# Bucket attention with a dense layer behind it: the first batch attended in one pass, its weights turned by TensorE's transpose

## The chip, the cores and the metric

The kernel runs on one core of a Trainium2 chip. The metric is the device time of one execution in microseconds (us). Three runs of the kernel before took 904.26, 904.30 and 908.95 us; their median is 904.3 us.

## What is computed

Four batches of eight heads, 768 tokens, 64 channels per head. A token sees only the tokens whose queries or keys fall into the same of 64 hash buckets; the attended values of all heads, 512 wide, go through a dense layer with GELU and a second dense layer.

```python
q_bits = (np.einsum('bhsd,dk->bhsk', q, proj) > 0)   # k_bits likewise, six bits each
mask = q_bucket[:, :, :, None] == k_bucket[:, :, None, :]
scores = np.where(mask, 0.125 * np.matmul(q, k.transpose(0, 1, 3, 2)), -1e9)
attn = np.exp(scores - np.max(scores, axis=-1, keepdims=True))
attn = attn / (np.sum(attn, axis=-1, keepdims=True) + 1e-09)
x = np.matmul(attn, v).transpose(0, 2, 1, 3).reshape(3072, 512)
h = x @ w_in                                         # 512 x 2048
return (0.5 * h * (1 + erf(h / sqrt(2)))) @ w_out    # 2048 x 512
```

## The kernel before

**Order of the work.** The kernel is a list of steps, each with an engine (or several to choose from), a cost, a key (smaller is sooner), the steps it needs and the buffer ring it takes. `Plan.order` (L94) simulates the engines and fixes the order in which each engine's instructions are written; the table `PAR` (L33) holds the numbers that shift the keys. At run time each engine works through its own list in that order and waits where a needed step is late.

**A unit** (`unit`, L748) is 128 queries of one head against all 768 keys; there are 192. TensorE (PE) makes the scores with four matmuls (L764), VectorE (DVE) takes the row maximum (L767) and the guarded scale (L771), ScalarE (ACT) the exponentials and their sum (L777), DVE the reciprocal (L786). Then the weights have to be turned, keys onto partitions, in one of two ways.

- *Half units*: the weights are split into two fp16 parts (L399 or L396 for the high part, L792 on DVE for the low part) and turned by a transposing DMA (L799). Their product with the values takes 36 fp16 matmuls per pair of heads and 256 queries (L889).
- *Whole units* (`whole_turn`, L823): a diagonal matrix of the reciprocals is made from the identity (tile `dr`), and six fp32 matmuls (L832) multiply each 128 x 128 block of weights with it, which turns and divides at once. Two copies bring the result from PSUM into `pt`. The product with the values takes 12 fp32 matmuls (L880).

**Passes.** Batch 0 is attended in two passes (`FIRST`, L24): all heads for the first 256 queries, then, heads in reverse, for the other 512. Three heads (`KEEP`) stay prepared between the passes; five are loaded and prepared a second time. `WHOLE` makes all four pairs of heads whole in the first pass and two in the second, so 32 units are whole and 160 half. A head's preparation (`head`, L642) loads q and k, splits them into high and low parts, projects them for the hash (L719 to L724) and writes the signs into rows of the operands. The weights of the dense layers are read, decoded on DVE from 64-bit floats (L488, L493, L498), scaled and split during batch 0. The scale of the values comes from four DVE maxima per batch (L589).

**Dense part.** Chunks of 256 tokens; per chunk two halves g of the 2048 hidden channels: 96 matmuls into the hidden (L1091) and 48 out of it (L1158) each. The list has all of a chunk's halves before the next chunk. In the first chunk the halves are drained into the result apart (`alone`, L1070), so that the first half can run before the weights of the second are there. Dense steps fill PE where attention leaves it free, and go on alone after the last unit.

```python
FIRST = (((0, 256),), ((256, 256), (512, 256)))
WHOLE = (4, 2, 0, 0, 0)
groups = [(b, ch, g) for b, chunks in passes for ch in chunks for g in range(NG)]
```

Of the kernel before, what the change touches and what calls it, by code (L numbers as in the profile page):

```python
# [10 lines left out]
F32 = mybir.dt.float32  # L11
# [8 lines left out]
P = 128  # L20
# [12 lines left out]
PAR = dict(DR_ACT=-376.07, DR_DVE=289.34, SI0=-278.25, SI1=416.6, SI2=306.7, SI_ACT=509.76, SI_DVE=47.66, SI_Pool=-124.88, Z=203.87, VS0=-105.38, H0=492.56, HL=-258.56, VS=-598.47, G2=553.48, HQ=415.51, VQ=-319.5, in0=576.69, out0=43.64, in1=45.59, out1=-9.06, in2=355.85, out2=56.84, in3=-68.45, out3=9.31, H1=322.83, H2=284.27, H3=-599.77, H4=-314.36, H5=134.87, H6=-600, H7=-32.98, MEV=599.38, MGE=18.26, MSP=118.02, V0=600, QK0=-74.85, QK1=593.04, QK2=76.57, MX0=-331.22, MX1=-185.25, MX2=-453.28, EX0=-301.14, EX1=-117.73, EX2=94.64, NR0=-107.13, NR1=-107.34, NR2=-398.77, HI0=584.08, HI1=-88.77, HI2=215.64, LO0=-593.61, LO1=-36.26, LO2=394.43, PV0=336.47, PV1=233.76, PV2=-154.35, TR0=-587.53, TR1=-414.23, TR2=158.02, V1=-484.38, V2=-573.42, Sin0=304.53, Sin1=397.8, Sin2=24.49, Sin3=-283.57, Sout0=471.96, Sout1=295.43, Sout2=26.22, Sout3=336.14, Lin=-221.37, Pin=-423.65, Qin=587.63, Cin=107.98, Min=438.2, Lout=-519.34, Pout=-600, Qout=-600, Cout=-600, Mout=578.13, G0=109.59, G1=-596.66, G3=-600, G4=-600, G5=-286.31, G6=-363.67, G7=-231.43, DUP0=-165.96, DUP1=326.7, DUP2=-339.67, LOW0=420.82, LOW1=-261.59, LOW2=-577.83, PRJ0=282.56, PRJ1=-69.75, PRJ2=-89.26, MSK0=456.41, MSK1=238.81, MSK2=501.82, DI_ACT=-410.83, DI_DVE=252.78, DI_Pool=-258.86, WS_ACT=-29.21, WS_DVE=-440.66, WS_Pool=490.46, WH_ACT=181.51, WH_DVE=-447.36, WH_Pool=-599.06, WL_ACT=70.41, WL_DVE=214, WL_Pool=283.28, VH_ACT=203.1, VH_DVE=477.67, VH_Pool=-442.09, MV_SP=97.35, MV_ACT=338.88, MV_DVE=-2.69, MV_Pool=-599.57, LO_ACT=301.58, LO_DVE=265.1, LO_Pool=-475.84, RND_ACT=-398.89, RND_DVE=200.27, RND_Pool=-52.67, MSK_ACT=48.02, MSK_DVE=-6.3, MSK_Pool=587.68, HI_ACT=-301.94, HI_DVE=128.62, HI_Pool=-390.82, DG_ACT=-447.94, DG_DVE=-318.17, DG_Pool=490.83, EV_ACT=140.3, EV_DVE=-346.2, EV_Pool=-344.6, GH_ACT=361.7, GH_DVE=587.31, GH_Pool=-257.89)  # L33
HOPX = {"PE": 0.0, "DVE": -0.1, "ACT": 0.14, "Pool": 0.1, "SP": 0.93}
# [188 lines left out]
def tile_bucket_attention_moe(  # L223
# [33 lines left out]
        "s": 2, "hp": 4, "p": 2, "hl": 2, "raw": 1, "rawe": RAWE, "sign": 1, "dr": 2, "pt": NTH + 1,  # L257
        "x": NTH, "vraw": 1, "vhl": 2, "wraw": 3, "o": 1, "diag": 1, "h": 1,
# [4 lines left out]
    def ring(pool, name, shape, dtype, count, first=0):  # L263
# [13 lines left out]
        "x": ring(const, "x", [P, 2, NPAIR, TC], F16, 1) + [None] * (2 * NTH - 1),  # L277
# [60 lines left out]
    make_identity(nc, ident)  # L338
    ones = const.tile([P, P], BF16, tag="ones", name="ones")
# [121 lines left out]
    def weight_pair(name, srcs, dsts, spare, clear, inv, key, step):  # L461
# [76 lines left out]
        for f, dst in zip(fs, dsts):  # L538
            box = []

            def scaled(f=f, box=box):
                affine(
                    box[0].engine, buf(box[0]).rearrange("p (c f) -> p c f", c=n), f.bitcast(F32), t[:, 2:3]
                )

            def high(dst=dst, box=box):
                affine(box[1].engine, dst[:, 0], buf(box[0]).rearrange("p (c f) -> p c f", c=n))

            def low(dst=dst, box=box):
# [694 lines left out]
```

## Time and profile before

| | before |
|---|---|
| median of three runs | 904.3 us |
| profiled execution: its time / its span | 907.79 / 906.0 us |
| PE busy | 865.1 us, 95% |
| DVE busy | 693.8 us, 77% |
| ACT busy | 618.9 us, 68% |
| GpSimd (POOL) busy | 275.4 us, 30% |
| granted TensorE clock, mean | 0.987 of 2.4 GHz |

The profile shows one execution. Busy shares are averages over stages that differ: the table by stretches among the rows below splits them. "Idle before, releaser" says how long an engine stood before an instruction and what it waited for. An instruction's duration in the list of groups includes its way through the pipeline; how fast PE really goes is read from the distance of starts in the timeline.

### The profile page before, as it was taken

The page shows a single profiled execution, that of the slowest core. Times are in us where ns is not written, and L with a number is a line of the kernel's source. Part 1 is how long each engine was busy: PE and PEld are TensorE (multiplying, and loading weights), DVE is VectorE, ACT ScalarE, POOL GpSimd, SP SyncE. Part 2 cuts the span into 40 slices and gives each one's busy share as a digit, 9 for nine tenths or more (in the row PEclk, how much of TensorE's full clock was granted, in tenths as well). Part 3 has the DMA queues.
Part 4 walks back from the last instruction along what each step waited for, and adds up shares of the span by engine and source line. Part 5 has one row for each costly group of instructions (what it writes and reads, how often), then busy time and mean ns, then how long its engine had stood idle before and what let it go on. Part 6 is the DMA issues. An engine that isn't in the chain of part 4 may idle for free. (4 is left out here: it accounts for less than half of the span.)

```text
span 906.0 us, 17437 instructions
## 1 busy us (share of the span) xinstructions
PE 865.1 (95%) x6592; PEld 630.8 (70%) x6592; DVE 693.8 (77%) x1334; ACT 618.9 (68%) x1028; POOL 275.4 (30%) x282
## 2 busy tenths in 40 slices
PE   4779999799999999999999999999999999999997
PEld 3557878565776867678776766777776757676663
DVE  7899999999999999998999998899994121212112
ACT  5777879878798888887888779878875323232231
POOL 6441134535455333333543324443510000000000
PEclk9969999899999999999999999999999999999999
DMA  8754563769989889997998988999796000000000
GB/s 255 229 161 153 182 219 90 141 140 185 193 197 205 160 204 204 178 184 156 209 182 198 203 158 181 174 194 162 159 162 100 25 11 14 24 1 25 1 24 24
DMA packets 299973, 128.30 MB, mean 142 GB/s; under 512 B 254064, under 2 KB 281840, under 8 KB 299888
## 3 DMA queue, kind: packets, MB, share of 16 engines
q1 hardware_dynamic: 299712, 127.17, 64.7%
q8 instruction: 52, 0.85, 0.4%
q14 instruction: 33, 0.27, 0.1%
q10 hardware_dynamic: 176, 0.00, 0.0%
HBM read 45.49 MB, written 6.29 MB: 57 GB/s over the span
## 5 line engine op out<-in xcount | busy, mean ns | idle before, releaser
L1091 PE MATMUL hp<-x,Win 128*128 128x256 f16 x2304 | 269.4, 274 | 0.0
L1158 PE MATMUL hp<-Wout,g 128*128 128x512 f16 x1152 | 265.6, 380 | 0.0
L1091 PEld LDWEIGHTS <-Win 128*128 128x128 f16 x2304 | 220.8, 98 | 43.3 <-issue 12.8
L1158 PEld LDWEIGHTS <-g 128*128 128x128 f16 x1152 | 107.5, 98 | 125.0 <-issue 10.4
L767 DVE TENSOR_REDUCE s<-s 128x1 f32<-128x768 f32 x192 | 180.8, 955 | 6.9 <-PE s L764 6.1
L777 ACT ACTIVATE p<-s,rows 128x768 f32<-128x768 f32 x141 | 139.2, 987 | 31.9 <-DVE rows L771 17.2
L764 PE MATMUL s<-Ak,Aq 128*128 128x384 f32 x352 | 139.4, 396 | 14.0 <-ACT p L777 8.5
L1101 ACT ACTIVATE h<-hp,ffs 128x512 f32<-128x512 f32 x96 | 65.6, 684 | 120.7 <-PE hp L1091 120.5
L1139 DVE SCALAR_TENSOR_TENSOR g<-h,ffs,g 128x512 f16<-128x512 f32 x96 | 71.4, 760 | 71.6 <-ACT g L396 68.1
L764 PE MATMUL s<-Bk,Bq 128*128 128x384 f32 x352 | 121.6, 345 | 0.0
L764 PEld LDWEIGHTS s<-Ak,Aq 128*128 128x128 f32 x352 | 68.5, 195 | 38.9 <-ACT p L777 14.1
L889 PE MATMUL hp<-pt,vhl 128*64 128x256 f16 x1440 | 85.5, 274 | 1.0 <-DVE x L916 1.0
L399 DVE TENSOR_SCALAR g<-h,ffs 128x512 f16<-128x512 f32 x36 | 19.5, 541 | 86.6 <-PE hp L1158 80.8
L889 PEld LDWEIGHTS <-vhl 128*64 128x64 f16 x1440 | 76.1, 110 | 11.8 <-issue 10.8
L764 PEld LDWEIGHTS s<-Bk,Bq 128*128 128x128 f32 x352 | 69.0, 196 | 1.0
L792 DVE SCALAR_TENSOR_TENSOR wbits<-p,rows,wbits 128x768 f16<-128x768 f32 x63 | 65.8, 1052 | 1.5 <-ACT wbits L396 0.7
L419 POOL TENSOR_TENSOR Bk<-raw,Aq 64x768 fp32r<-64x768 f32 x30 | 58.6, 1953 | 26.0 <-ACT Aq L396 20.8
L399 POOL TENSOR_SCALAR rows<-rows 128x1 f32<-128x1 f32 x57 | 23.3, 408 | 114.5 <-ACT p L777 72.3
L777 ACT ACTIVATE wbits<-s,rows 128x768 f32<-128x768 f32 x51 | 50.4, 988 | 10.2 <-DVE rows L771 6.8
L832 PE MATMUL hp<-dr,p 128*128 128x128 f32 x384 | 51.7, 288 | 3.1 <-ACT dr L396 2.3
L832 PEld LDWEIGHTS hp<-dr,p 128*128 128x128 f32 x384 | 48.1, 200 | 8.4 <-ACT dr L396 4.4
L727 ACT ACTIVATE sign<-hp,off 44x256 f32<-44x256 f32 (+1 forms) x74 | 41.6, 571 | 16.7 <-PE hp L724 16.3
(161 smaller groups left out, 1198.2 us busy)
## 6 DMA issues: line engine op xcount, KB each, us to landing
raw<-qk SPq DMA_DIRECT2D x33, 384.0 KB, 4.0
vraw<-v SPq DMA_DIRECT2D x30, 384.0 KB, 4.1
wbits<-w_in SPq DMA_DIRECT2D x16, 512.0 KB, 4.4
wbits<-w_out SPq DMA_DIRECT2D x16, 512.0 KB, 4.2
out<-o SPq DMA_DIRECT2D x12, 512.0 KB, 3.5
Ak<-Aq SPq DMA_DIRECT2D x24, 192.0 KB, 3.4
Bk<-Aq SPq DMA_DIRECT2D x19, 192.0 KB, 3.2
vhl<-v SPq DMA_DIRECT2D x6, 384.0 KB, 5.1
```

The costliest lines, as they stand in the source:

```text
L399: on.tensor_scalar(out=out, in0=in_, scalar1=scale, scalar2=bias, op0=ALU.mult, op1=ALU.add)
L419: on.tensor_tensor(out=out, in0=in0, in1=in1, op=ALU.subtract)
L764: nc.tensor.matmul(to, x, y, start=k == 0, stop=k == 1)
L767: nc.vector.tensor_reduce(out=buf(sp)[:, SPARE + 1 : SPARE + 2], in_=both(sp), axis=AX.XY, op=ALU.max, negate=True)
L777: nc.scalar.activation(out=buf(ex).rearrange("p (b k) -> p b k", b=2), in_=both(sp), func=AF.Exp, scale=sc, bias=nb, accum_out=ssum,)
L792: nc.vector.scalar_tensor_tensor(out=buf(hi)[:, 1], in0=buf(ex), scalar=r, in1=buf(hi)[:, 0], op0=ALU.mult, op1=ALU.subtract,)
L832: nc.tensor.matmul(buf(step[0])[:, (k - k0) * P : (k - k0 + 1) * P], buf(ex)[:, words(k)], buf(dg), start=True, stop=True,)
L889: nc.tensor.matmul(pv[j * D : (j + 1) * D], buf(vh)[:, tv, kt, j * D : (j + 1) * D], buf(holds[j][0])[:, tp * KT + kt, :nt], start=kt == 0 ...
L1091: nc.tensor.matmul(buf(pair[0])[:, j * ch[1] : (j + 1) * ch[1]], win_hl[:, f0 // WB1, tw, pr, f0 % WB1 : f0 % WB1 + P], x[:, tx, pr, : ch[1]],
L1101: nc.scalar.activation(out=bufs["h"][0][:, 2 * fp : 2 * fp + 2, :nt], in_=buf(pair[0])[:, : 2 * nt].rearrange("p (j k) -> p j k", j=2), fu ...
L1139: nc.vector.scalar_tensor_tensor(out=gt[:, 1, s2, :nt], in0=h[:, s2, :nt], scalar=sg, in1=gt[:, 0, s2, :nt], op0=ALU.mult, op1=ALU.subtract,)
L1158: nc.tensor.matmul(buf(banks[u]), gt[:, tg, f, u * P : (u + 1) * P], wout_hl[:, ft // UT, tw, ft % UT], start=fresh and f == ti == 0, stop ...
```

## The change

- Batch 0 is attended in one pass like the others: each of its heads is prepared once, for all 768 queries, with one extra set of operands (`NEARLY` 2 to 1). All its four pairs are whole: 48 units are whole, 144 half.
- A whole unit no longer makes a diagonal. The weights are divided in place (768 wide, on ACT, POOL or DVE), and six TensorE transposes with an fp32 identity turn them (L833 of the new file).
- The scale of batch 0's values comes from the squares of the values, 24 bf16 matmuls on PE (L596) and one small maximum, in place of four DVE maxima.
- The dense halves of the first two chunks take turns: half 0 of chunk 0, half 0 of chunk 1, half 1 of chunk 0, half 1 of chunk 1 (`APART`). The result ring `o` has two buffers instead of one, and the rescaled weights wait in `wraw` instead of `o`.
- `PAR` and `HOPX` have new numbers, so the order is new on every engine.

```diff
-FIRST = (((0, 256),), ((256, 256), (512, 256)))
-NEARLY = 2
+NEARLY = 1
-KEEP = 3
-WHOLE = (4, 2, 0, 0, 0)
+WHOLE = (4, 0, 0, 0)
+TURN = 0.1
+APART = 2
...
-PAR = dict(DR_ACT=-376.07, DR_DVE=289.34, SI0=-278.25, SI1=416.6, SI2=306.7, ...
+PAR = dict(DR_ACT=180.03, DR_DVE=32.78, SI0=-234.76, SI1=321.18, SI2=-274.91, ...
...
+        def squares(pr, box):
+            up = raw(box[0]).rearrange("p c d -> p (c d)").bitcast(BF16).rearrange("p (c d t) -> p c d t", c=KT, t=2)
+            for c in range(KT):
+                x = up[:, c, :, 1]
+                nc.tensor.matmul(
+                    buf(parts[0])[:, :P], x, x, start=pr == c == 0, stop=pr == NPAIR - 1 and c == KT - 1
+                )
...
-        def diagonal():
-            affine(dg.engine, buf(dg), ident, r)
+        def divided():
+            affine(dg.engine, buf(ex), buf(ex), r)
 
         def product(k0, k1, step):
             for k in range(k0, k1):
-                nc.tensor.matmul(
-                    buf(step[0])[:, (k - k0) * P : (k - k0 + 1) * P], buf(ex)[:, words(k)], buf(dg),
-                    start=True, stop=True,
+                nc.tensor.transpose(
+                    buf(step[0])[:, (k - k0) * P : (k - k0 + 1) * P], buf(ex)[:, words(k)], ident32,
                 )
...
-        dg = add(affine_on("DG", P, True), 0, diagonal, t + PAR[f"HI{cl}"], [nr], takes="dr", port=True)
+        dg = add(affine_on("DG", S, True), 0, divided, t + PAR[f"HI{cl}"], [nr], port=True)
...
-    for n_pass, (b, chunks) in enumerate(passes):
...
+    for b in range(B):
+        v_ready[b] = v_scale(b, t - PAR["VS"] if b else PAR["VS0"])
+        n_sets = NSET if b else NSET + 1 + NEARLY
...
-    groups = [(b, ch, g) for b, chunks in passes for ch in chunks for g in range(NG)]
+    apart = chunks[:APART]
+    groups = [(0, ch, g) for g in range(NG) for ch in apart]
+    groups += [(b, ch, g) for b in range(B) for ch in chunks[0 if b else APART :] for g in range(NG)]
...
-        alone = n < NG
-        k = n if alone else NG + b
+        alone = n < NG * APART
+        k = g if alone else NG + b
```

How the order moves is seen at three places. The first is PE's list in the middle of batch 0, before (L832 the turning by the diagonal `dr`, L764 scores, L880 the fp32 product with the values; "x3" are three matmuls).

```order
L832 MATMUL hp_64<-dr_117,p_68 128x128 x3
L832 MATMUL hp_66<-dr_117,p_68 128x128 x3
L880 MATMUL hp_65<-pt_75,vhl_81 64x256
L880 MATMUL hp_65<-pt_76,vhl_81 64x256
L880 MATMUL hp_65<-pt_75,vhl_81 64x256
L880 MATMUL hp_65<-pt_76,vhl_81 64x256
L764 MATMUL s_63<-Ak_89,Aq_88 128x384
L764 MATMUL s_63<-Bk_91,Bq_90 128x384
```

The same place in the changed kernel (L833 the transposes, L765 scores, L880 as before).

```order
L833 MATMUL hp_64<-ident_128,p_69 128x128 x3
L833 MATMUL hp_65<-ident_128,p_69 128x128 x3
L765 MATMUL s_62<-Ak_88,Aq_87 128x384
L765 MATMUL s_62<-Bk_90,Bq_89 128x384
L765 MATMUL s_62<-Ak_88,Aq_87 128x384
L765 MATMUL s_62<-Bk_90,Bq_89 128x384
L880 MATMUL hp_66<-pt_73,vhl_83 64x256
L880 MATMUL hp_66<-pt_74,vhl_83 64x256
```

The identity stands where the diagonal stood; the steps follow each other as before, but all of batch 0's 48 units pass this way, and 32 did.

The second place is PE's list where the dense part begins. Before (L1091 into the hidden, L434 a small spread of a maximum), it begins between the scores of the 30th and of the 31st unit, in the second pass; the rows are those around the 31st.

```order
L1091 MATMUL hp_66<-x_77,Win 128x256
L764 MATMUL s_62<-x_104,x_103 128x384
L764 MATMUL s_62<-x_105,rest 128x384
L764 MATMUL s_62<-x_104,x_103 128x384
L764 MATMUL s_62<-x_105,rest 128x384
L434 LDWEIGHTS ones
L434 MATMUL hp_64<-diag_83,ones 128x128
L1091 LDWEIGHTS Win
```

In the changed kernel (L1074) the first dense matmul comes behind the scores of the 48th unit, the last of batch 0 (the first two rows are its scores, two of four).

```order
L765 MATMUL s_63<-Ak_113,Aq_112 128x384
L765 MATMUL s_63<-Bk_115,Bq_114 128x384
L880 MATMUL hp_67<-pt_74,vhl_83 64x256
...
L833 MATMUL hp_65<-ident_128,p_69 128x128 x3
L833 MATMUL hp_64<-ident_128,p_69 128x128 x3
L432 LDWEIGHTS ones
L432 MATMUL hp_67<-diag_86,ones 128x128
L1074 LDWEIGHTS Win
L1074 MATMUL hp_66<-x_77,Win 128x256
```

PE thus has no dense work to fill gaps with until the scores of all of batch 0 are made, where before it had some from two thirds on.

The third place is DVE's list shortly before that, in the changed kernel (L768 maximum, L772 guarded scale, L787 reciprocal, L397 a copy of turned weights, L486 and L491 decoding of dense weights, L688 the low part of a head's q).

```order
L768 TENSOR_REDUCE s_62<-s_62 128x1
L688 SCALAR_TENSOR_TENSOR Bq_89<-raw_80,Aq_87 64x768
L787 RECIPROCAL rows<-rows 128x1
L772 SCALAR_TENSOR_TENSOR rows<-limit,s_62 128x2
L768 TENSOR_REDUCE s_63<-s_63 128x1
L397 TENSOR_SCALAR Aq_112<-sign_72 12x768
L772 SCALAR_TENSOR_TENSOR rows<-limit,s_63 128x2
L397 TENSOR_SCALAR pt_75<-hp_67 128x3x128
L486 TENSOR_SCALAR Win<-wbits 128x512
```

Before, the 33rd maximum stands in this manner (L767, L771, L786 as the three above, L558 the low part of scaled dense weights, L680 the low part of q, 512 wide in the second pass).

```order
L558 SCALAR_TENSOR_TENSOR Wout<-Win,tiny,Wout 128x1024 x2
L389 RECIPROCAL tiny<-inv_97 128x1
L680 SCALAR_TENSOR_TENSOR Bq_86<-raw_78,Aq_84 64x512
L399 TENSOR_SCALAR rows<-rows 128x1
L786 RECIPROCAL rows<-rows 128x1
L767 TENSOR_REDUCE s_63<-s_63 128x1
L786 RECIPROCAL rows<-rows 128x1
L558 SCALAR_TENSOR_TENSOR Win<-Win,tiny 128x1024
L771 SCALAR_TENSOR_TENSOR rows<-limit,s_63 128x2
```

Decoding and splitting of dense weights are stretched over more units than before: between two maxima stands less of them.

## Rows read from the trace of the kernel before

**Rows 1.** Stretches: length, busy PE, PEld, DVE, ACT, POOL (instructions); PEclk; DMA share, GB/s.

```profile
0.00:147.00 147.00, 121.92 (x863) 98.27 (x864) 136.05 (x301) 109.27 (x217) 54.60 (x62) 0.94 0.62 191
147.00:209.00 62.00, 55.30 (x413) 40.40 (x412) 60.04 (x112) 51.25 (x84) 28.98 (x25) 0.94 0.68 135
209.00:316.00 107.00, 103.81 (x845) 76.55 (x843) 103.60 (x194) 89.49 (x150) 50.67 (x49) 1.00 0.94 189
316.00:906.00 590.00, 584.05 (x4478) 415.61 (x4476) 394.10 (x730) 368.92 (x579) 141.14 (x148) 1.00 0.60 121
```

**Rows 2.** The row maxima (L767) alone, from the start: their number (x) by then.

```profile
0.00:147.00 147.00, 30.59 (x33) 0.94 0.62 191
0.00:209.00 209.00, 44.91 (x48) 0.94 0.64 174
0.00:316.00 316.00, 74.97 (x80) 0.96 0.74 179
```

**Rows 3.** PE's timeline at 2.4 GHz: start, duration, operation (products have two records each).

```profile
30.33 1.60 PE L832 MATMUL hp<-dr,p 128*128 128x128 f32 x12 [1.51 <-ACT dr L396]
31.70 0.42 PE L764 MATMUL s<-x,x 128*128 128x384 f32 x1
31.95 0.34 PE L764 MATMUL s<-x,rest 128*128 128x384 f32 x1
32.13 0.33 PE L764 MATMUL s<-x,x 128*128 128x384 f32 x1
...
107.50 0.62 PE L510 MATMUL hp<-Wout 128*128 128x128 bf16 x8
107.95 0.62 PE L510 MATMUL hp<-Win 128*128 128x128 bf16 x8
...
152.75 2.81 PE L880 MATMUL hp<-pt,vhl 128*64 128x256 f32 x24
155.49 0.44 PE L764 MATMUL s<-Ak,Aq 128*128 128x384 f32 x1
```

**Rows 4.** Chain of work that ended last, long pieces: start, length, what.

```profile
544.31 4.05 PE hp L889 x72
736.73 9.71 PE hp L1158 x45
788.13 10.48 PE hp L1091 x96
```

**Rows 5.** DVE groups: operation, count, busy us, mean ns of one, idle before.

```profile
L767 DVE TENSOR_REDUCE s<-s 128x1 f32<-128x768 f32 x192 | 180.8, 955 | 6.9 <-PE s L764 6.1
L771 DVE SCALAR_TENSOR_TENSOR rows<-limit,s 128x2 f32<-128x2 f32 x192 | 38.6, 216 | 0.8
L399 DVE TENSOR_SCALAR pt<-hp 128x384 f32<-128x384 f32 x19 | 10.4, 551 | 3.4 <-PE hp L832 3.2
L792 DVE SCALAR_TENSOR_TENSOR hl<-p,rows,hl 128x768 f16<-128x768 f32 x46 | 48.0, 1045 | 0.4 <-issue 0.2
L498 DVE SCALAR_TENSOR_TENSOR Wout<-wbits,Wout 128x512 int32<-128x512 int32 x20 | 15.5, 785 | 0.0
L493 DVE SCALAR_TENSOR_TENSOR Wout<-wbits,Wout 128x512 int32<-128x512 int32 x20 | 13.6, 686 | 0.1
L488 DVE TENSOR_SCALAR Wout<-wbits 128x512 int32<-128x512 int32 x20 | 8.9, 452 | 0.0
```

**Rows 6.** PE's timeline where the granted clock was 1.2 GHz.

```profile
50.58 0.69 PE L764 MATMUL s<-Ak,Aq 128*128 128x384 f32 x1 [1.78 <-ACT Ak L396]
51.06 0.52 PE L764 MATMUL s<-Bk,Bq 128*128 128x384 f32 x1
51.38 0.52 PE L764 MATMUL s<-Ak,Aq 128*128 128x384 f32 x1
```

**Rows 7.** ACT and POOL groups of the whole units' turning.

```profile
L396 ACT ACTIVATE dr<-ident,rows 128x128 f32<-128x128 bf16 x25 | 10.0, 400 | 9.1 <-DVE rows L786 8.9
L396 ACT ACTIVATE wbits<-p,rows 128x768 f16<-128x768 f32 x30 | 28.0, 932 | 7.1 <-DVE rows L786 5.7 <-ACT h L1101 0.6 <-ACT sign L727 0.5
```

More of the change, by code (lines that the diff above doesn't have):

```diff
@@ L35 @@
+HOPX = {"PE": -0.03, "DVE": -0.1, "ACT": 0.12, "Pool": 0.27, "SP": 1.04}
 BIG = 2.0**34
@@ L599, in v_scale @@
             )
+            if b == 0:
+                parts.append(
+                    add(
+                        "PE", 0.36, lambda pr=pr, box=box: squares(pr, box), key, [box[0], *parts[-1:]],
+                        takes=None if pr else "hp",
+                    )
+                )
+                free(box[0], [parts[-1]])
+                continue
             parts.append(add("DVE", 0.87, lambda pr=pr, box=box: biggest(pr, box), key, [box[0]]))
@@ L605, in one @@
         def one():
-            nc.vector.tensor_reduce(out=t[:, 0:1], in_=stat_v[:, b], axis=AX.X, op=ALU.max)
-        sc = everywhere(t, add("DVE", 0.07, one, key, parts), key)
-        return add_scale(key, sc, t, inv_v[:, b : b + 1], s_v[:, b : b + 1])
+            of = buf(parts[0])[:, :P] if b == 0 else stat_v[:, b]
+            nc.vector.tensor_reduce(out=t[:, 0:1], in_=of, axis=AX.X, op=ALU.max)
+        top = add("DVE", 0.2 if b == 0 else 0.07, one, key, parts)
+        if b == 0:
+            free(parts[0], [top])
+        sc = everywhere(t, top, key)
+        return add_scale(key, sc, t, inv_v[:, b : b + 1], s_v[:, b : b + 1], b == 0)
     def values_whole(b, pr, key):
@@ L685, in add_low @@
             if scale:
[L686 removed]
+                return add("DVE", subtract_cost("DVE", S), scaled, key + PAR[f"LOW{cl}"], [hi], port=True)
             box = []
@@ L689, in add_low @@
                 add(
-                    subtract_on("LO", n), 0,
-                    lambda: subtract(box[0].engine, out, buf(raw)[rows, cols], aq[rows, cols].bitcast(F32)),
+                    subtract_on("LO", S), 0,
+                    lambda: subtract(box[0].engine, out, buf(raw)[rows], aq[rows].bitcast(F32)),
                     key + PAR[f"LOW{cl}"], [hi], port=True,
@@ L842, in copy @@
             )
-        dg = add(affine_on("DG", P, True), 0, diagonal, t + PAR[f"HI{cl}"], [nr], takes="dr", port=True)
+        dg = add(affine_on("DG", S, True), 0, divided, t + PAR[f"HI{cl}"], [nr], port=True)
+        if not hold:
+            hold.append(add("none", 0, lambda: None, -10, [dg], takes="pt"))
         prods, copies = [], []
@@ L848, in whole_turn @@
             step.append(
-                add("PE", 0.223 * (k1 - k0), lambda k0=k0, k1=k1, step=step: product(k0, k1, step), t + PAR[f"LO{cl}"], [dg], takes="hp")
+                add("PE", TURN * (k1 - k0), lambda k0=k0, k1=k1, step=step: product(k0, k1, step), t + PAR[f"LO{cl}"], [dg, hold[0]], takes="hp")
             )
@@ L853, in whole_turn @@
                 lambda k0=k0, k1=k1, step=step: copy(step[1].engine, k0, k1, step),
-                t + PAR[f"TR{cl}"], [step[0], *hold[:1]], takes=None if hold else "pt",
+                t + PAR[f"TR{cl}"], step[:1],
             )
             step.append(done)
-            hold.append(done)
             free(step[0], [done])
@@ L930, in values @@
         return parts[-1]
-    whole = tuple((c, TC) for c in range(0, S, TC))
-    passes = [(0, chunks) for chunks in FIRST] + [(b, whole) for b in range(1, B)]
+    chunks = tuple((c, TC) for c in range(0, S, TC))
     xt, x_parts = {}, {}
     early_steps = []
-    last_use = {}
-    used, owner = {}, {}
+    last_use, used = {}, {}
     v_ready = {}
```

145 lines of the change are left out of this document (52 added, 93 removed).

## The prediction

> **What bounds the kernel now.** I read the busy time by stretch first, then the row maxima as a clock of progress, then the timeline and the groups for prices. The stretches [rows 1] show three stages. To 147 us DVE is busy 136.1 us, 93%, and PE 121.9; from 147 to 209 DVE is busy 97% and PE 89%; from 209 to 316 both stand at 97%; behind 316 PE is busy 584 of 590 us and DVE 394. So VectorE sets the pace while batch 0 is attended and the dense weights are decoded, and TensorE sets it for the rest. The maxima [rows 2] count the units: 33 by 147 us, 48 (all of batch 0) by 209 us, 80 by 316 us. I price a stage by the instructions that its lists hold, and take the slower of the two engines.
>
> **How PE's list is priced.** The counts are those of the order, the prices distances of starts at 2.4 GHz [rows 3]: six fp32 turning products in 1.37 us (30.33 to 31.70), 0.228 us each; a score matmul 0.175 (four of them 0.70), with 0.08 more where the kind of work changes (31.70 to 31.95 is 0.25); 12 fp32 products with values 2.74 us (152.75 to 155.49); eight bf16 matmuls 128 wide 0.45, 0.056 each. Dense and fp16 work from the chain [rows 4]: 96 into the hidden in 10.48 (0.109), 45 out of it in 9.71 (0.216), 72 fp16 products with values in 4.05 (0.056). Priced so, the list of before is 865 us long, against a span of 906: 41 us are lost, nearly all before the 80th unit, and behind that the list needs 597 us where 590 passed, a factor of 0.988.
>
> **How DVE's list is priced.** By the means of the groups [rows 5], of which the largest: a maximum 0.955, a guarded scale 0.216, a copy of turned weights 0.551, a half block of dense weights decoded in 0.785 + 0.686 + 0.452 = 1.92, a low part of a half unit 1.05. Up to the 33rd maximum its list holds 33 maxima (31.5), 32 scales (6.9), 18 copies (9.9), 28 half blocks (53.8) and 53.9 us of the rest, 156.0 in all. It was busy 136.1 (instructions overlap, factor 0.872) and idle 10.9, most of it at the start.
>
> **The change, part by part, on PE.** Removed: 192 turning products (43.6), five second preparations of heads: five projections each, at the scores' rate (384 columns in 0.175) 0.94 together, less the 0.24 by which the first ones get wider, so 3.5 for five. Four times a pair with 256 queries goes from 36 fp16 to 12 fp32 products: -8 and +11. Added: 24 squares at 0.056 (1.4), 1.1 of changes of kind, and 288 transposes. No transpose on PE is in the trace. Below it is bounded by the bf16 matmul of the same width, 0.056; above by the fp32 product on the same block, 0.228. I take 0.113, half of the product, since that has two records per matmul and moves the block in both; it is the row with the same operand and shape. 288 of them are 32.5 us. Sum: the list falls from 865.2 to 856.4 us, by 8.8.
>
> **On the other engines.** A diagonal (0.40 on ACT) becomes a division 768 wide (0.93 for such an activation [rows 7]); ACT has 27 of these, POOL 21, DVE two. Sixteen units give up a high part, a low part of 1.05 on DVE [rows 5] and a transposing DMA; 64 copies become 96, of which DVE has 30 (19 before). The buffer of exponentials, two deep, is held for the division and the transposes, 0.93 + 0.68, where it was held for diagonal and products, 0.40 + 1.37: no longer than before. Five head loads with their moves leave the queue of SP; the 16 DMA engines were busy 62% to 147 us [rows 1], so a load that moves a few places is no bound there. Four maxima over the values leave DVE; what waits for the squares on PE is only their buffer's next load. The second result buffer lets a drain of one chunk pass the store of another; in the tail PE is busy anyway, so I cost it at nothing.
>
> **Stage A, to the 48th maximum.** The new list of DVE holds 48 maxima (45.8), 47 scales (10.2), 28 copies (15.4), 24 half blocks (46.1) and 56.4 of the rest: 173.9. By the factor and the idle time above: 173.9 x 0.872 + 10.9 = 162.5 us, where before the 48th came at 209. PE's list up to there is 118.5 us, without any dense work; with the 25 us that it was idle to 147 [rows 1] that is 143.5, less than DVE needs. So the transposes, 264 of which lie here, run beside DVE: their price is hidden up to (162.5 - 25 - 88.7) / 264 = 0.185 us. ACT's list is 151.8 us; by its factor (109.3 busy for a list of 126.1) 132, also hidden.
>
> **Stage B, to the 80th.** DVE's list is 155.1 us (114.4 before), since eight half blocks (15.4) and their scaling are left over, and the dense halves come in at once. Its factor there was 103.6 / 114.4 = 0.906: 140.5 us. PE's list is 133.7, times 0.988 132. So DVE sets the end again, and PE loses 8 us: 303 us at the 80th maximum, against 316. By then PE's list of before has done 267.8 us, that of the change 252.2.
>
> **Stage C, the rest.** 856.4 - 252.2 = 604.2 us of PE's list, times 0.988: 597 us, against 590. Sum 162.5 + 140.5 + 597 = 900 us of span, against 906: 6 us less. The profiled execution took 907.8 with what lies around the span; it becomes 902. The median of the runs shown, 904.3, is 3.5 us below it, and I subtract the same 6: **898 us**.
>
> **The rivals.**
> - *PE is never held in stage B* (890 us). DVE's factor in stage A is 0.872; with it the 155.1 us would be 135, about PE's 132, and the 8 us fall away. For it: decoding, of short factor, is what is added there. Against: before, 0.906 stood with fewer small instructions.
> - *The transposes don't do what they are there for* (912 us). At the fp32 product's 0.228 stage A's list on PE is 149, with the 25 idle 174, 11 us over DVE, and the 24 later ones add 3. For it: data, identity and width are those of the product. Against: one record less. The Trainium skill, page "TensorE: Matmul & The Clock Gate", Part 4 (PE-mode transpose), gives about 275 ns for a 128 x 128 transpose in a kernel; by that the sum would be some 926. No run here shows it, and it is no end of my range.
> - *The clock falls in stage A and it gets slower* (918 us). In the trace the score matmuls go from 0.175 us apart to 0.32 (51.06 to 51.38) at 1.2 GHz, behind a wait of 1.78 us [rows 6]; the mean granted clock to 209 us is 0.94 [rows 1]. Before, PE was busy 83% to 147 us with dense work and heavy products; now its list fills 118.5 of 162.5. Each us of list at 1.2 GHz costs 0.83 more. It decides from 19 / 0.83 = 23 us of list on; with 47 us, two fifths, it is +39 - 19 = 20. Against: the stage has no long waits but at the start, and the lighter the list, the more a slow clock is hidden. The same section of the Trainium skill says that transposes do not hold the clock at its full level as matmuls do; by that rule this rival would be the likely one. No run here shows it: the trace of before has no transpose on PE.
> - *Decoding is late for the dense part* (905 us). From 147 to 209 PE was idle 6.7 us [rows 1]; if the first dense halves wait as long again for weights, nearly all of the gain goes. Against: half 0 of two chunks asks only for the first half of the weights, twice as much work for the same weights.
>
> **How the numbers follow.** A measurement of this kernel tells about 0.5%, 4.5 us, from no change: faster is below 899.8, slower above 908.8. The forecast has 0.40, with a spread of 893 to 904 from 0.03 in DVE's factors (5 us each): 0.24 of it faster, 0.16 within. PE never held, 0.20, faster. Late decoding, 0.12, within. Dear transposes, 0.12, and the clock, 0.16, slower. Together: faster 0.44, same 0.28, slower 0.28. The range reaches from the first rival's lower part, 886, to the clock's 919.
>
> **What would show it.** In the new profile: the 48th maximum at 157 to 168 us and the 80th at 298 to 308; transposes about 0.11 us apart; DVE busy over 93% up to the 80th; PE's idle time about 44 us, all before that; the last maximum near 733 us, since 688 us of PE's new list stand ahead of it and the dense tail gets shorter. Wrong would be: PE's granted clock at 1.2 GHz for more than 25 us behind the first 40; transposes further than 0.185 apart; or waits of dense matmuls for decoded weights of over 8 us. Then the step of stage A or B fails, not the price of the rest.

## The result and the profile after

| | before | changed |
|---|---|---|
| median of six runs beside each other | 904.84 us (904.26 to 909.35) | 898.80 us (897.61 to 900.83) |
| ratio, 95% interval | 1 | 0.9912 [0.9885, 0.9939] |
| profiled execution: time / span | 907.79 / 906.0 us | 900.17 / 898.1 us |
| PE busy / idle | 865.1 / 40.9 us | 855.6 / 42.5 us |
| granted clock, mean | 0.987 | 0.992 |

The changed kernel is faster by 0.9%; forecast were 898.0 us and a gain of 6. Measured once more, beside the last three experiments, it had 901.04 us where the kernel before had 906.69: 0.9935 [0.991, 0.9961].

The first view is the busy time by stretch, now cut at the 48th and at the 80th row maximum, and behind these two more stretches, for the clock. Columns: stretch, its length, then PE, PE's weight loads, DVE, ACT and POOL busy with their counts, granted clock, DMA share, GB/s.

```profile
0.00:157.00 157.00, 129.90 (x874) 92.15 (x876) 148.98 (x331) 130.34 (x255) 74.25 (x86) 0.98 0.57 169
157.00:301.20 144.20, 136.79 (x1073) 101.04 (x1070) 137.00 (x268) 113.76 (x180) 41.34 (x40) 0.98 0.61 128
301.20:898.10 596.90, 588.86 (x4509) 417.30 (x4507) 409.36 (x741) 390.92 (x616) 110.24 (x113) 1.00 0.59 119
...
28.00:163.00 135.00, 120.68 (x868) 85.66 (x868) 131.82 (x306) 118.12 (x240) 59.72 (x65) 1.00 0.50 145
188.40:195.30 6.90, 6.11 (x21) 4.31 (x22) 6.21 (x16) 4.62 (x10) 3.02 (x4) 0.51 0.41 110
```

Stage A ends at 157.0 us (208.8 before), stage B takes 144.2 more, stage C 596.9. DVE is busy 95% in A and in B; PE loses 27.1, 7.4 and 8.0 us in the three stages. Counted as in [rows 2], the maxima stand thus in the same view, of L768 alone (only DVE's busy time is shown):

```profile
0.00:147.00 147.00, 41.96 (x44) 0.98 0.59 174
0.00:209.00 209.00, 55.22 (x58) 0.97 0.55 155
0.00:316.00 316.00, 80.83 (x85) 0.98 0.62 152
```

44 units are started by 147 us where 33 were [rows 2], 58 against 48 by 209, 85 against 80 by 316. The lead shrinks from 52 us to 15 between the 48th and the 80th unit, since the dense work that the kernel before did within batch 0 now comes here, and it turns round at the end: the 192nd maximum is at 727.3 us, 47 us later than before, and the purely dense tail behind it takes 171 us where it took 225.

The transposes in PE's timeline (start, length, engine, line, tile, count, wait before):

```profile
59.82 0.87 PE L833 MATMUL hp<-ident,p 128*128 128x128 f32 x6
60.45 0.42 PE L765 MATMUL s<-x,x 128*128 128x384 f32 x1
...
186.81 0.32 PE L726 MATMUL hp<-Bq,hash_hi 128*44 128x256 f32 x1 [3.43 <-DVE Bq L688]
...
189.19 0.69 PE L765 MATMUL s<-Ak,Aq 128*128 128x384 f32 x1 [1.18 <-ACT p L778]
189.67 0.52 PE L765 MATMUL s<-Bk,Bq 128*128 128x384 f32 x1
189.99 0.52 PE L765 MATMUL s<-Ak,Aq 128*128 128x384 f32 x1
```

Six transposes take 0.63 us from their first start to the next instruction's (59.82 to 60.45), 0.105 each, where six products took 1.37 [rows 3]. The last rows lie at the start of the only spell at 1.2 GHz behind the first 28 us (188.4 to 195.3, granted clock 0.51): before it and at its start PE waits 3.43 us for the low part of a query of batch 1 that stands in DVE's list behind other low parts, then 1.18 more, and the scores are 0.32 apart as in [rows 6].

The groups of PE in stage B (line, engine, operation, tiles, form, count, then busy us and mean ns, then idle time before them and its releasers):

```profile
L1074 PE MATMUL hp<-x,Win 128*128 128x256 f16 x436 | 51.7, 276 | 0.8 <-DVE tiny L529 0.8
...
L726 PE MATMUL hp<-Bq,hash_hi 128*44 128x256 f32 (+1 forms) x8 | 2.7, 343 | 3.4 <-DVE Bq L688 3.4
```

The dense matmuls waited 0.8 us in all for anything of the weights. So the gain is PE's: 9.5 us less busy, 1.6 us more idle, 7.9 us of span. Not all of the 9.5 us is a shorter list. PE stood at 1.2 GHz for about 24 us in the profile before and for about 14 in this one; the rows lie within these spells, first the two of before, then the two of the changed kernel.

```profile
46.30:63.20 16.90, 11.87 (x48) 9.28 (x47) 15.79 (x28) 11.76 (x21) 7.46 (x7) 0.50 0.48 140
172.60:179.30 6.70, 6.07 (x24) 4.84 (x25) 6.54 (x12) 5.36 (x9) 5.63 (x6) 0.50 0.45 91
...
21.20:27.90 6.70, 5.63 (x19) 4.49 (x20) 4.98 (x13) 5.70 (x10) 4.71 (x4) 0.50 0.75 218
188.50:195.20 6.70, 6.01 (x21) 4.21 (x22) 6.01 (x16) 4.42 (x10) 2.92 (x4) 0.50 0.42 112
```

PE was busy 17.9 us in them before and 11.6 now. Scores are 0.32 us apart there and 0.175 at 2.4 GHz [rows 3], [rows 6], so the 6.3 us less are worth 6.3 x (1 - 0.175 / 0.32) = 2.9 us: by this estimate some 3 of the 9.5 us are the clock's. The spells differ between executions too; a second profile of the changed kernel (experiment 6) has one more, of 3.4 us at 116 us.

### The profile page after: what moved, and what is told of

The parts are those of the page before. It is cut to its first block, busy times and chain, and to the rows that moved or that the text cites. A ratio compares the mean times of both kernels' runs of the same rounds, so it can differ in the third digit from the quotient of the medians.

```text
span 898.1 us, 17035 instructions
## 1 busy us (share of the span) xinstructions
PE 855.6 (95%) x6452; PEld 610.5 (68%) x6452; DVE 695.3 (77%) x1337; ACT 635.0 (71%) x1050; POOL 225.8 (25%) x239
## 4 chain that ended last, share of the span: by engine, by line
PE 75%; DVE 16%; ACT 5%; issue 2%; DMA 1%; SPq 0%; POOL 0%; DVEq 0%; ACTq 0%
PE hp L1141 25%; PE hp L1074 24%; PE s L765 12%; PE hp L889 8%; DVE s L768 4%; ACT p L778 2%; PE hp L880 1%; PE hp L833 1%; DVE Bq L688 1%; PE hp L725 1%; PE hp L727 1%; DVE hl L793 1%; DMA Bk<-Aq 1%; PE hp L726 1%; DVE wbits L793 1%
## 5 line engine op out<-in xcount | busy, mean ns | idle before, releaser
L1074 PE MATMUL hp<-x,Win 128*128 128x256 f16 x2304 | 267.5, 273 | 0.8 <-DVE tiny L529 0.8
L1074 PEld LDWEIGHTS <-Win 128*128 128x128 f16 x2304 | 220.7, 98 | 41.2 <-issue 12.3
L768 DVE TENSOR_REDUCE s<-s 128x1 f32<-128x768 f32 x192 | 181.7, 959 | 16.1 <-PE s L765 14.1
L778 ACT ACTIVATE p<-s,rows 128x768 f32<-128x768 f32 x148 | 145.9, 987 | 21.9 <-DVE rows L772 14.1
L765 PE MATMUL s<-Ak,Aq 128*128 128x384 f32 x360 | 141.7, 394 | 11.4 <-ACT p L778 9.5
L765 PE MATMUL s<-Bk,Bq 128*128 128x384 f32 x360 | 123.3, 343 | 0.0
L1122 DVE SCALAR_TENSOR_TENSOR g<-h,ffs,g 128x512 f16<-128x512 f32 x96 | 75.2, 796 | 48.2 <-ACT g L394 43.4
L765 PEld LDWEIGHTS s<-Ak,Aq 128*128 128x128 f32 x360 | 69.2, 192 | 36.4 <-ACT p L778 23.1
L397 DVE TENSOR_SCALAR g<-h,ffs 128x512 f16<-128x512 f32 x42 | 21.2, 505 | 75.1 <-PE hp L1141 60.6
L889 PE MATMUL hp<-pt,vhl 128*64 128x256 f16 x1296 | 76.3, 274 | 1.7 <-DVE vhl L650 1.6
L889 PEld LDWEIGHTS <-vhl 128*64 128x64 f16 x1296 | 68.7, 110 | 11.1 <-issue 9.2
L765 PEld LDWEIGHTS s<-Bk,Bq 128*128 128x128 f32 x360 | 69.6, 193 | 1.0
L793 DVE SCALAR_TENSOR_TENSOR wbits<-p,rows,wbits 128x768 f16<-128x768 f32 x56 | 60.0, 1074 | 2.4 <-ACT wbits L394 2.1
L397 POOL TENSOR_SCALAR rows<-rows 128x1 f32<-128x1 f32 x50 | 20.0, 401 | 162.0 <-ACT p L778 89.6
L417 POOL TENSOR_TENSOR Bk<-raw,Aq 64x768 fp32r<-64x768 f32 x24 | 45.6, 1900 | 36.6 <-ACT Aq L394 35.2
L833 PE MATMUL hp<-ident,p 128*128 128x128 f32 x288 | 42.6, 282 | 8.1 <-POOL p L397 2.7
L778 ACT ACTIVATE wbits<-s,rows 128x768 f32<-128x768 f32 x44 | 43.3, 984 | 8.5 <-DVE rows L772 7.1
L793 DVE SCALAR_TENSOR_TENSOR hl<-p,rows,hl 128x768 f16<-128x768 f32 x44 | 45.9, 1051 | 1.0 <-POOL hl L397 0.7
L1108 ACT ACTIVATE h<-h 128x2048 f32<-128x2048 f32 x24 | 45.9, 1911 | 0.4
```

What stands on the lines that cost most here:

```text
L417: on.tensor_tensor(out=out, in0=in0, in1=in1, op=ALU.subtract)
L765: nc.tensor.matmul(to, x, y, start=k == 0, stop=k == 1)
L768: nc.vector.tensor_reduce(out=buf(sp)[:, SPARE + 1 : SPARE + 2], in_=both(sp), axis=AX.XY, op=ALU.max, negate=True)
L778: nc.scalar.activation(out=buf(ex).rearrange("p (b k) -> p b k", b=2), in_=both(sp), func=AF.Exp, scale=sc, bias=nb, accum_out=ssum,)
L793: nc.vector.scalar_tensor_tensor(out=buf(hi)[:, 1], in0=buf(ex), scalar=r, in1=buf(hi)[:, 0], op0=ALU.mult, op1=ALU.subtract,)
L833: nc.tensor.transpose(buf(step[0])[:, (k - k0) * P : (k - k0 + 1) * P], buf(ex)[:, words(k)], ident32,)
```

## The experiments

Two times of the changed kernel stand above; the runs below are held against the mean of its two ratios, 0.9924, in us of the kernel before (907 on these chips). The intervals of both sides make such a difference uncertain by some 2 to 3 us. The ends of the stages are read from one profile each, and they scatter as well: in the two profiles of the changed kernel stage A took 157.0 and 159.0 us, stage B 144.2 and 142.9, stage C 596.9 both times. Runs that were timed beside the changed kernel itself are compared with that.

**1. Load on one engine in one stage.** Theory: DVE sets the end of stage A, PE of stage C. Four runs add work to the one or the other, the rest of the order as it is.

```diff
-            nc.vector.scalar_tensor_tensor(
+            for _ in range(2 if t // 48 == 0 else 1):   # batch 3: == 3
+                nc.vector.scalar_tensor_tensor(
...
                 to = buf(sp)[:, j * 512 : j * 512 + S // 2]
+                if t // 48 == 0:                        # batch 3: == 3
+                    nc.tensor.matmul(to, aq[:, qs], ak[:, n], start=True, stop=True)
                 for k, (x, y) in enumerate(((aq[:, qs], ak[:, n]), (bq[:, qs], bk[:, n]))):
```

The guarded scale twice, in batch 0 and in batch 3:

> The changed kernel, its guarded scale (216 ns on DVE) made twice in each of batch 0's 48 units; same order. My theory, DVE sets the pace until batch 0 is attended: 48 x 0.216 = 10.4 us, times the overlap factor 0.872, so about 9 us slower than the changed kernel (908 against 899), the 48th maximum at 166 us instead of 157. Rival, PE bounds the kernel everywhere: 0 to 2 us.

> The same doubling in batch 3's 48 units alone. My theory, PE sets the end there and DVE is idle a sixth of that stretch: 0 to 2 us. Rival, DVE bounds wherever there is attention: about 9 us, as in batch 0.

Two more score matmuls per unit, written over by those that follow, in batch 0 and in batch 3:

> The changed kernel with one of the two score matmuls per half made twice in batch 0's units (96 more, 0.175 us each, 16.8 us of PE); same order. My theory: PE's list is lighter than DVE's there and most of it is hidden, 0 to 4 us. Rival, PE bounds everywhere: 16.8 us.

> The same 96 additional matmuls in batch 3's units. My theory, PE-bound: 16 to 17 us slower, 915 to 916. Rival, attention bound by DVE there too: 0 to 5 us.

| run | ratio, 95% interval | against the changed kernel |
|---|---|---|
| scale twice, batch 0 | 1.0027 [1.0012, 1.0041] | +9 us of 10.4 added |
| scale twice, batch 3 | 0.9959 [0.9944, 0.9974] | +3 us of 10.4 |
| scores more, batch 0 | 0.9985 [0.9968, 1.0002] | +6 us of 16.8 |
| scores more, batch 3 | 1.0080 [1.0056, 1.0104] | +14 us of 16.8 |

The stretch up to the 48th maximum, first with the scale twice, then (another kernel) with more scores:

```profile
0.00:168.30 168.30, 134.43 (x882) 93.19 (x882) 161.49 (x379) 132.02 (x255) 73.00 (x86) 0.97 0.54 158
```

```profile
0.00:163.40 163.40, 142.02 (x964) 107.67 (x966) 151.59 (x332) 130.96 (x255) 72.64 (x86) 1.00 0.55 162
```

In batch 0 work on DVE appears in full: stage A is 11 us longer, DVE busy 12.5 more. That is more than the 10.4 added, since the decoding steps of the stage take 49.2 us there and 44.4 in the changed kernel (experiment 3 shows why they can). Work on PE appears in part: stage A is 6 us longer, PE busy 12 more and idle 21.4 where 27.1 was. Of the 16.8 us added an estimated 2.6 came back, since the spell at 1.2 GHz from 21 us on, with 5.7 us of PE's work in it, is not there (granted clock 1.00 in the row). In batch 3 it is the other way round: PE's 16.8 us lengthen stage C by 15. The theory holds as to which engine leads in stages A and C; no run adds work in stage B alone. Both cross terms, +6 and +3, are above what the theory said (0 to 4, 0 to 2), by no more than their uncertainty. That the other engine is not far behind, and a delay of one unit reaches it, would explain them; it is not shown.

**2. The transposes taken back to products,** in the changed kernel's order:

```diff
-                nc.tensor.transpose(
+                nc.tensor.matmul(
                     buf(step[0])[:, (k - k0) * P : (k - k0 + 1) * P], buf(ex)[:, words(k)], ident32,
+                    start=True, stop=True,
```

> The changed kernel, its 288 transposes made as fp32 products with the same identity; same order. A transpose was measured 0.105 us from the next, the product 0.228: 264 x 0.123 = 32.5 us more of PE ahead of the 48th unit, 3 us behind. My theory, hidden under DVE as far as PE is idle there (26 us to the 48th maximum, some 10 of them at the start that nothing can fill): 9 to 19 us slower, 908 to 918. Rival A, PE bounds: 35 us, 934. Rival B, all hidden: 0 to 3 us.

920.86 us, ratio 1.0142 [1.0114, 1.0171]: +20 us, just above the upper end of the theory (19). In its trace twelve records, six products, go from 68.74 to 70.10, 0.227 us each:

```profile
68.74 1.60 PE L833 MATMUL hp<-ident,p 128*128 128x128 f32 x12
70.10 0.42 PE L765 MATMUL s<-x,x 128*128 128x384 f32 x1
```

Its groups of DVE up to the 48th maximum, and behind them the same two of the changed kernel:

```profile
L768 DVE TENSOR_REDUCE s<-s 128x1 f32<-128x768 f32 x48 | 45.9, 960 | 5.9 <-PE s L765 5.8
L397 DVE TENSOR_SCALAR pt<-hp 128x384 f32<-128x384 f32 x28 | 15.6, 556 | 10.6 <-PE hp L833 9.5 <-ACT pt L394 0.7
```

```profile
L768 DVE TENSOR_REDUCE s<-s 128x1 f32<-128x768 f32 x48 | 45.8, 957 | 3.2 <-PE s L765 3.1
L397 DVE TENSOR_SCALAR pt<-hp 128x384 f32<-128x384 f32 x28 | 15.3, 551 | 0.9 <-PE hp L833 0.7
```

Now DVE waits 10.6 us for the turned weights where it waited 0.9, and the 48th maximum comes at 176.4 us. With products PE is the longer engine of stage A.

**3. The transposes alone,** put into the kernel before with its two passes and its own order:

```diff
-            affine(dg.engine, buf(dg), ident, r)
+            affine(dg.engine, buf(ex), buf(ex), r)
...
-                nc.tensor.matmul(
-                    buf(step[0])[:, (k - k0) * P : (k - k0 + 1) * P], buf(ex)[:, words(k)], buf(dg),
-                    start=True, stop=True,
+                nc.tensor.transpose(
+                    buf(step[0])[:, (k - k0) * P : (k - k0 + 1) * P], buf(ex)[:, words(k)], ident32,
```

> The kernel before with the transposes alone: its 32 whole units are divided in place and turned by transposes, everything else and the order as before. PE's list gets 32 x (1.37 - 0.63) = 24 us shorter, all of it ahead of 176 us where DVE is busy 93 to 97%; ACT's gets 13 us longer. My theory, DVE sets the pace there: 0 to 6 us faster than before (899 to 905). Rival, the cheaper turning is where the gain comes from: 20 to 24 us faster, 881 to 885.

912.44 us, ratio 1.0045 [1.003, 1.006]: slower than before by 4 us; both expectations fell. The stretch up to the 48th maximum, of the kernel before and then of this one:

```profile
0.00:208.80 208.80, 177.02 (x1272) 138.57 (x1273) 195.88 (x412) 160.31 (x300) 83.51 (x86) 0.94 0.64 174
```

```profile
0.00:212.30 212.30, 158.90 (x1075) 111.04 (x1076) 200.24 (x412) 170.16 (x300) 86.86 (x87) 0.94 0.62 171
```

PE's busy time falls by 18 us and its idle time rises by 22 (from 31.8 to 53.4): all that the transposes save stands idle, because DVE leads. And DVE, with the same 412 instructions, is busy 4.4 us longer, about as much as the kernel loses. The decoding accounts for it: its six groups take 65.6 us in the stage where they took 61.3, and most of that is in one, 586 ns here where it was 452 [rows 5]:

```profile
L490 DVE TENSOR_SCALAR Wout<-wbits 128x512 int32<-128x512 int32 x20 | 11.6, 586 | 0.4 <-DMA wbits<-w_in 0.4
```

and the timelines of DVE and of POOL show one of these steps beside a division:

```profile
98.50 0.41 DVE L490 TENSOR_SCALAR Win<-wbits 128x512 int32<-128x512 int32 x1
98.82 0.68 DVE L500 SCALAR_TENSOR_TENSOR Win<-wbits,Win 128x512 int32<-128x512 int32 x1
99.42 1.05 DVE L490 TENSOR_SCALAR Wout<-wbits 128x512 int32<-128x512 int32 x1
...
100.46 0.94 DVE L769 TENSOR_REDUCE s<-s 128x1 f32<-128x768 f32 x1
```

```profile
98.75 1.45 POOL L401 TENSOR_SCALAR p<-p,rows 128x768 f32<-128x768 f32 x1 [5.19 <-PE s L766]
100.28 1.88 POOL L421 TENSOR_TENSOR x<-raw,x 64x768 fp32r<-64x768 f32 x1
```

The step at 99.42 takes 1.05 us, not 0.41: POOL's division ends at 98.75 + 1.45 = 100.20 and the step at 100.47. All six steps of this kind that took over 0.7 us in the stage end 0.27 to 0.29 us behind the end of an instruction of POOL that began before them, while the row maximum, which reads PSUM, takes its 0.94 us beside POOL at 100.46. So a decoding step is mostly held until POOL is through, but not always: of the ten of this kind that begin within an instruction of POOL nine end 0.28 to 0.29 us behind it, and the tenth, at 188.16, takes its 0.42 us and ends 0.65 us ahead of it; the step at 98.82, of another kind, begins 0.07 us into the division above and takes its usual 0.68. Of the six long ones, two stand behind a division that was a diagonal before, three behind parts of a head's preparation and one behind a dense step. It seems to be less the wider instruction than the shift of the whole stage that brings more of them together; no run separates the two, nor takes the waits away. The kernel before has such steps too (its mean of 452 ns [rows 5] is above the 0.41 us at 98.50).

**4. Dense halves chunk by chunk again,** the order drawn anew by the planner:

```diff
-APART = 2
+APART = 1
```

> The changed kernel with the dense halves chunk by chunk again (APART 1); the order is drawn up anew by the same numbers. If taking turns matters, dense matmuls of the second half wait for decoded weights between 160 and 260 us: 4 to 10 us slower, 903 to 909. Rival, the turns are not where the gain comes from: within 3 us of the changed kernel.

908.37 us, ratio 1.0006 [0.9987, 1.0024]: +7 us, the size that was expected. Its stretches of the same three stages, and the largest wait of PE in stage B:

```profile
0.00:158.20 158.20, 130.51 (x874) 93.10 (x876) 149.36 (x331) 130.42 (x255) 73.90 (x86) 0.98 0.57 168
158.20:303.10 144.90, 130.61 (x1007) 95.41 (x1004) 131.89 (x260) 111.59 (x177) 43.99 (x40) 0.95 0.65 135
303.10:906.90 603.80, 598.39 (x4575) 422.93 (x4573) 412.19 (x761) 378.59 (x592) 108.81 (x111) 1.00 0.59 120
```

```profile
L889 PE MATMUL hp<-pt,vhl 128*64 128x256 f16 x216 | 14.8, 296 | 6.9 <-ACT vhl L394 6.3 <-DVE vhl L650 0.6
```

Stage B is as long as in the changed kernel, with 66 matmuls fewer in it: PE is idle 14.3 us there instead of 7.4, and stage C is 6.9 longer by the work left over. The granted clock of the stage is 0.95 instead of 0.98: within the wait of 6.3 us a second spell at 1.2 GHz begins, from 227.2 to 234.1 us. The wait that was expected, of dense matmuls for decoded weights, is not in the trace: the matmuls into the hidden wait 0.7 us in stage B, and not for weights. What grew is a wait for the values of batch 1, and the drawn order differs in many places. So that the turns of the halves are the cause is open.

**5. The scale from squares.** Once more of it (batch 1 too, order drawn anew), then none of it (four DVE maxima in the places of the squares, order kept):

```diff
-            if b == 0:
+            if b <= 1:
```

> The changed kernel with the scale of batch 1's values from squares too: four maxima of 0.944 us off DVE where DVE is short, 24 small matmuls (1.4 us) on PE; order drawn up anew. My theory: 1 to 2 us faster, 897, if the new order is as good; rival, the order, fitted to the list of the change, loses more than that: 2 to 8 us slower.

```diff
-            for c in range(KT):
-                x = up[:, c, :, 1]
-                nc.tensor.matmul(
...
+            biggest(pr, box)
```

> The scale of batch 0's values again from four maxima on VectorE, 0.95 us each, in the places of the squares; no instruction else changes its place. VectorE gets 3.8 us of work within the first 40 us, TensorE loses 1.4. Theory (VectorE sets the pace of stage A from its start, each us there costs one): 2 to 4 us slower than the changed kernel. Rival (the first maxima lie in VectorE's waits for loads, and nothing is to be had from the squares): within 1.5 us.

For two batches: 906.06 us, 0.9982 [0.9964, 1.0001], +5 us; for none: 901.9 us, 0.9946 [0.9926, 0.9967], beside the changed kernel's 901.04 and 0.9935, no difference. The first, as its rival said, shows what a new drawing of the order can cost here: its 48th maximum is at 165.1 us. Four maxima fewer are asked of DVE, but it is busy 155.6 us up to there, as the planner gave it 40 copies of turned weights (28 before) and other parts of the dense weights ahead of it. Its stretch of stage A, and the group:

```profile
0.00:165.10 165.10, 133.67 (x892) 92.98 (x894) 155.64 (x349) 129.31 (x244) 76.33 (x88) 0.98 0.52 157
```

```profile
L397 DVE TENSOR_SCALAR pt<-hp 128x384 f32<-128x384 f32 x40 | 21.2, 551 | 1.0 <-PE hp L833 0.9
```

The second says that the squares themselves are worth nothing that can be measured: beside the changed kernel's second profile DVE is busy 3.5 us longer in stage A, and as much less idle.

**6. DVE relieved.** If DVE leads in stage A, taking work from it should pay. First the step that adds 1e-9 to the sum goes from batch 0, then also half of DVE's copies go to ACT. The first run is the changed kernel itself, beside the other two.

```diff
-            affine(su.engine, si, ssum, unity, 1e-9 * unity)
+            if not whole:
+                affine(su.engine, si, ssum, unity, 1e-9 * unity)
...
-            nc.vector.reciprocal(out=r, in_=si)
+            nc.vector.reciprocal(out=r, in_=ssum if whole else si)
...
         def copy(on, k0, k1, step):
+            if on == "DVE":                 # the second kernel alone
+                moved[0] += 1
+                on = "ACT" if moved[0] % 2 else on
```

> The changed kernel, nothing altered, as the base for the runs beside it. Expected: ratio to the kernel before 0.988 to 0.994, some 899 us where the kernel before takes 907.

> In batch 0 the reciprocal is taken of the sum itself: the step that adds 1e-9 (27 on ScalarE at 0.20 us, 12 on GpSimd at 0.40, 8 on VectorE at 0.15) goes, all else stays in its place. Since the sum is at least 1, the value in fp32 is the same. Theory (VectorE bounds stage A): 1 us less from VectorE's eight, so 0 to 2 us faster than the changed kernel. Rival (the chain from the exponentials to the transposes holds TensorE, or ScalarE is the bound): the chain is 0.3 to 0.8 us shorter for each of 48 units, ScalarE's list by 5.4 us: 4 to 8 us faster.

> As no_sum_step, and every second copy of turned weights that VectorE made (15 of 30, 0.55 us each) goes to ScalarE (0.49 each) in the same place of the order: VectorE's list of stage A falls by 8 us, ScalarE's rises by 7 less the 5.4 of the sums. Theory (VectorE bounds stage A, each us counts): 4 to 9 us faster than the changed kernel, the 48th maximum at 149 to 153 us where it came at 157. Rival (TensorE or ScalarE is the bound as soon as VectorE gives way, as the 6 of 17 us that more scores cost hints at): 0 to 2 us faster, with VectorE idle longer before the maxima.

901.04, 902.19 and 899.78 us; ratios 0.9935 [0.991, 0.9961], 0.9946 [0.993, 0.9962] and 0.9922 [0.9905, 0.994]. The sum's step alone is worth nothing that can be measured. With the copies the kernel is 1.3 us faster than the changed one by the medians, and 2.4 faster than without the sum's step, which the intervals do not tell from none; 1.3 lies where the rival said, not the theory. In the profiles the 48th maximum comes at 159.0, 159.9 and 155.9 us. The decoding steps of DVE in stage A, of the changed kernel measured again, then of the run without the sum's step, then of the last:

```profile
L486 DVE TENSOR_SCALAR Win<-wbits 128x512 int32<-128x512 int32 x12 | 5.5, 466 | 0.0
L486 DVE TENSOR_SCALAR Wout<-wbits 128x512 int32<-128x512 int32 x12 | 5.0, 426 | 0.0
```

```profile
L486 DVE TENSOR_SCALAR Win<-wbits 128x512 int32<-128x512 int32 x12 | 6.8, 574 | 0.0
L486 DVE TENSOR_SCALAR Wout<-wbits 128x512 int32<-128x512 int32 x12 | 6.6, 560 | 0.0
```

```profile
L769 DVE TENSOR_REDUCE s<-s 128x1 f32<-128x768 f32 x48 | 45.8, 959 | 4.3 <-PE s L766 3.9 <-issue 0.2
...
L398 DVE TENSOR_SCALAR pt<-hp 128x384 f32<-128x384 f32 x14 | 7.7, 553 | 0.8 <-PE hp L835 0.8
L487 DVE TENSOR_SCALAR Wout<-wbits 128x512 int32<-128x512 int32 x12 | 7.4, 620 | 0.0
L487 DVE TENSOR_SCALAR Win<-wbits 128x512 int32<-128x512 int32 x12 | 6.3, 532 | 0.0
```

DVE's list lost 8.5 us (14 copies, 7.5, and seven sums, 1.0), but 3.2 came back in decoding steps that now begin while POOL is at work and are held, and its busy time fell by 3.4 only. Nearly all of the 3.2 (2.9) is there when the sum's step alone is gone, so it is not the moved copies that bring it. The 48th maximum comes 3.1 us earlier than in the second profile of the changed kernel, about what DVE's busy time lost, and 1.1 earlier than in the first. DVE stands idle 4.3 us before the maxima where it was 3.1. This kernel has the lowest median of the four timed beside each other, not measurably below the changed one.

## Why the prediction was right

**The sum, stage by stage.** Forecast 162.5 + 140.5 + 597, measured 157.0 + 144.2 + 596.9. Stage C was right to 0.1 us: PE's list times 0.988. In stage A the factor of DVE was 149.0 / 173.9 = 0.857 instead of 0.872 (2.6 us) and its idle time 8.0 instead of 10.9 (2.9). In stage B the working left the idle time out: of 144.2 us DVE was idle 7.2, its factor was 137.0 / 155.1 = 0.883, and the forecast's 0.906 stood for both. The two misses, -5.5 and +3.7 us, have opposite signs, so that the total comes nearer than its parts is luck. Of the signs it named, the 48th maximum (157 to 168) lies on the edge of its range, the 80th (298 to 308) within, and the last, meant for 733, came at 727.

**The transpose** was bounded by 0.056 and 0.228, taken at 0.113, and measured 0.105. The Trainium skill, page "TensorE: Matmul & The Clock Gate", Part 4, gives about 275 ns for one of 128 x 128 in a kernel. In this trace that is near the mean length of one record (282 ns for the 264 of stage A), its way through the pipeline included, and not the distance at which they follow each other.

```profile
L833 PE MATMUL hp<-ident,p 128*128 128x128 f32 x264 | 39.1, 282 | 7.9 <-POOL p L397 2.7 <-DVE x L914 1.9 <-DVE rows L772 1.2
```

**PE's list** was to shrink by 8.8 us; PE's busy time shrank by 9.5. That agrees in part by luck: some 3 of the 9.5 are the clock's by the estimate above, which leaves 6 to 7. (The terms of the working as printed add up to 9.1, not 8.8; and ACT was given 27 of the 48 divisions, of which it has 25. Neither matters to the sum.) PE's idle time was to be about 44 us and is 42.5, 34.5 of it before the 80th unit; the 8.0 behind it were contained in the factor 0.988, not seen as idle.

**DVE as the bound of stage A** was right as to the end that it sets (experiment 1) and too simple as a rule: work added to it costs about all of its time, 8.5 us of work taken from its list gave 1 to 3 us, and PE's work is hidden to a half or two thirds, where the working had room for 19 us of it. DVE's own length depends on POOL; that it is only the longest of several chains that are nearly equal is likely, not shown.

**The rivals.** *PE never held* did not come true: PE lost 7.4 us in stage B against 8 forecast, 3.4 of them in one wait for DVE. That DVE sets the end of this stage was not tested; both engines are busy 95% of it. *Dear transposes* was wrong by the price, and experiment 2 measures the rival itself: its stage A was worked out as 174 us and came at 176.4, but its total of 912 was 9 too low (920.9): 2.4 of it in stage A, 5.4 in stage B (145.9 us for the 140.5 of the working, which was short there with transposes too), less 1.6 in stage C; the last 3 are most likely the chips of these runs, where the kernel before took 907.6 us and not 904.3. *The clock* did not come true: from 28 to 163 us, where 270 of the 288 transposes run, the granted clock is 1.00. By the rule in the same section of the Trainium skill that transposes do not hold the full clock, it should have fallen there; this trace does not bear that out for transposes mixed with scores and products. The one spell behind the first 28 us is 7 us long, in stage B, and follows a wait. *Late decoding* did not come true: 0.8 us of waits for weights, 8 would have been needed.

**What the prediction did not see** is that the parts, in the orders that were run, pay only together. Transposes alone make the kernel before slower by 4 us (experiment 3), one pass with divisions in place and products is 13 slower than before (experiment 2, ratio 1.0142), and both together are faster by 6 to 8. One pass puts the turning of 48 units on PE in stage A where 32 were, and needs the cheap turn; the cheap turn gives PE time that only counts where DVE has less to do per unit. Both runs kept an order that was drawn for another kernel, and experiment 5 shows that an order not fitted can cost 5 us; how much of the 4 and of the 13 is that was not measured. The waits that they show, PE's behind DVE in the one and DVE's behind PE in the other, are of the size of the work that was taken away or added. A rival is left: the change also brings new numbers for the planner, and no run gives the kernel before a newly fitted order alone. How much of the 6 to 8 us is the order's is open.

## What to carry to other kernels

Price a change by stages, in each by the list of the engine that leads, and then ask for every saving whether that engine made it: 18 us less work on PE came back as 22 us of waiting where VectorE led. Where two engines stand at 83 and 95%, adding to the leader cost about all of it, while 8.5 us taken from its list gave 1 to 3: look afterwards at the leader's busy time, not at its list, and at what is next, before counting the gain. An instruction on GpSimd is not free beside VectorE: ask which of VectorE's instructions it can hold.

## What the runs showed of the hardware

- A 128 x 128 fp32 transpose on PE has one record and follows the last one after 0.105 us at 2.4 GHz, under half of the fp32 product of the same block (0.227, two records).
- A decoding step of DVE (128 x 512, int32, from SBUF to SBUF; L490 of experiment 3) takes 0.42 us alone. Of the ten there that begin while GpSimd is within an instruction, nine end 0.28 to 0.29 us behind that instruction's end, whatever is left of it: the one at 52.32 takes 2.06 us. The other two kinds of step (0.68 us alone) end 0.54 to 0.55 us behind when they are held. It is not always DVE that waits: the tenth step, at 188.16, takes its 0.42 us beside an instruction of GpSimd on 128 x 1 that is recorded with 1.24 us, where the mean of these in the changed kernel is 0.40. The Trainium skill, page "SBUF — State Buffer", section "SBUF: two separate sides", states that the two engines share a pair of ports as an exclusive lock, held for a whole instruction by the one that starts first; the rows agree. That such waits grow when a short step elsewhere goes (by 2.9 us without the sum's step, experiment 6) was not expected.
